# Pack attention and a channel mix on one core: a third softmax buffer, sums of weights stored in 2 KB runs, and later due times in the planner

## The chip, the cores and the metric

The kernel runs on one core of a Trainium2 chip. Its engines are TensorE (PE: matmuls, PEld: the weight loads that overlap them), VectorE (DVE), ScalarE (ACT), GpSimd (POOL) and SyncE (SP), which issues nearly all transfers. Each runs its own list of instructions in order and waits for the others by semaphores. The metric is the device time of one execution in microseconds.

## The reference

Two attentions in a row: 32 packed queries p attend to k and v, and q attends to the packed result; then a channel mix with a token shift.

```python
B, H, S, D, NP = 8, 8, 576, 64, 32;  d_model, d_ff = 512, 1024
def sm_attn(qq, kk, vv):
    s = scale * qq @ kk.transpose(0, 1, 3, 2)
    a = np.exp(s - s.max(-1, keepdims=True))
    return (a / (a.sum(-1, keepdims=True) + 1e-09)) @ vv
p_packed = sm_attn(p, k, v)
x = sm_attn(q, p_packed, p_packed)        # then (B, S, 512)
xk = mu_k * x + (1 - mu_k) * x_prev       # x_prev: x one token earlier
xr = mu_r * x + (1 - mu_r) * x_prev
v = np.maximum(xk @ w_k, 0) ** 2 @ w_v
out = v / (1 + np.exp(-(xr @ w_r)))
```

All is float32. The large products split each operand into a high and a low part and do three matmuls for one.

## The kernel before

**Stages.** Attention goes by the 8 batches of 576 rows, the channel mix by 9 blocks of 512 rows. Blocks 0 to 4 run one by one: 16 groups of gates (tiles `pr`, lines 1157 to 1159), 32 of keys (`ph`, 1090 to 1092), 32 of values (`pvo`, 1186 to 1188), where a group is three matmuls of 512 columns. Blocks 5 and 6, then 7 and 8 run as pairs (lines 1474 and 1628 to 1630): 32 groups of turned gates, then seven products instead of eight for keys and for values, 56 groups each. Those need sums of weights (`sw`), which are made on VectorE (line 1307) and ScalarE (1323) during blocks 1 to 4, stored to memory from `tmp` tiles (`sum<-sw`) and read back in the pairs into a ring of four cells: two in old k and q tiles (`ring`), two in columns of `wv_h` and `wv_l`.

**One batch of attention on PE.** Five kinds of short bursts go between groups: first scores (723, of `kT`), the product with v (745, into `pv`), the transposition of `pm` (775), second scores (879, of `qT`), and twice the last product (926, with `a`), whose result ScalarE copies into `xt` (949). Between the first scores and the product with v lies the first softmax: its exponentials are turned on VectorE into an `e` tile (`blocks`), stored (`away`) and read back (`aT`). Between second scores and last product lies the second softmax, in two halves, each in an `e` tile: turn (895), maximum (901), subtraction (903), exponential (905), sum (908), division (910 to 914), turn into `a` (918). k and q are loaded in pieces into `raw` tiles and turned on VectorE (455).

**What sets the order.** `Flow` is a planner that runs when the program is built. Each piece of work is a generator that asks for tiles (`take`, `give`), events, and time on an engine (`vec`, `act`, `pe`, `load`). Flow keeps a clock for each engine and emits next what could start earliest by its own costs, and among equals the lowest rank. The emitted order is fixed; on the chip an engine waits at an instruction until its inputs are there. The table `RANK_...` sets ranks, `BUFS` the number of tiles. `LANDS` (2.0) is the time that the planner adds to a transfer, `flow.t` the time at which a piece is ready by its clocks. A `tmp` tile (four) holds either a square on its way (`r`, 1102), a mixed `x` (1050), or a sum until its store has landed.

Of the kernel before, what the change touches and what calls it, by code (L numbers as in the profile page):

```python
# [182 lines left out]
def attn_pack_channel_mix(ctx: ExitStack, tc: tile.TileContext, q, k, v, p, mu_k, mu_r, w_k, w_v, w_r, out):  # L183
# [53 lines left out]
    def pe(us, after=None):  # L237
        return "tensor", us, after, None

    def load(dst, src, issue, us, queue="queue"):  # L240
        yield queue, issue, None, None
        dict(queue=nc.sync, scalar=nc.scalar, gpsimd=nc.gpsimd)[queue].dma_start(dst, src)  # L242
        begin = max(flow.free.get("dma", 0.0), flow.t + 0.46)
        flow.free["dma"] = begin + us
        flow.free[queue] = max(flow.free[queue], begin - 2.0)
        flow.now.t = begin + us + LANDS

    LANDS = 2.0
    T6 = S // 6
    HALVES = slice(0, 64), slice(64, P)  # L250

    def reached():
# [10 lines left out]
    ps = ctx.enter_context(tc.tile_pool(name="ps", bufs=1, space=bass.MemoryType.PSUM))  # L263
    pairs = ctx.enter_context(ExitStack())
    pp = pairs.enter_context(tc.tile_pool(name="pp", bufs=1, space=bass.MemoryType.PSUM))
    BUFS = dict(raw=3, kq=4, vt=2, pt=1, a0=1, a1=1, aT=1, pm=2, e=2, a2=1, xt=6, tmp=4, xk=NC, sq=NF, sig=4,
                pa=2, both=1, m=4, n=4, staged=4, ex=3, pair=0, ring=0, store=2, ahead=0)
    for tag, n in BUFS.items():
        flow.pool(tag, n)
    flow.slots["m"].pop()  # L270
# [3 lines left out]

    PAIRS = NB - 4, NB - 2
    MORE = {("sig", 4 + j): f"raw{j}" for j in range(3)}
    MORE.update({("sig", 7): "a20"})
    RANK_B, RANK_TURN, RANK_BACK, RANK_OUT, RANK_AHEAD, RANK_L = 4.805, 10.211, 4.545, 0.48, 25.869, 31.395
    RANK_SUMS, CHAIN, KEPT = dict(k=29.865, v=12.442), {NB - 4: 45, NB - 2: 37.468}, {NB - 4: 23.054, NB - 2: 6.114}

    def banks(slot):
        return pp.tile([P, 2, 512], F32, name="pa", tag=f"pa{slot}")
# [5 lines left out]
            const.tile([P, 1 if "m" == tag[0] or "n" == tag[0] else 2], F32, name=f"{tag}{j}", tag=f"{tag}{j}")  # L288
    for tag, n, size in (
        ("xk", NC, 2 * TB), ("sq", NF, 2 * TB), ("tmp", 4, WP), ("sig", 4, DM), ("kq", 4, S),   # L290
        ("raw", 3, S), ("a2", 1, S), ("ex", 3, TB), ("e", 2, S), ("aT", 1, 5 * P), ("vt", 2, NPR * 5 * D),
    ):
        for j in range(n):
            sb.tile([P, size], F32, name=tag, tag=f"{tag}{j}")
# [88 lines left out]
    def first_loads():  # L383
        flow.spawn(first_packed(), 5)
        for h in range(2):
            for j in (2 * h, 2 * h + 1):
                flow.spawn(first_pair(k, "kT", j, "xk"), FIRST_K[h])
                flow.spawn(first_pair(q, "qT", j, "xk" if j == NPR - 1 else "raw"), FIRST_Q[h])
            flow.spawn(values_of(0, h), FIRST_V[h])

    def loads(b):
        flow.spawn(packed(b), lrank(b) - 0.03)
        for src, tag in ((k, "kT"), (v, "vt"), (q, "qT")):
            if tag == "vt":
                for h in range(2):
                    flow.spawn(values_of(b, h), lrank(b) - 0.01)
                continue
            flow.now.rank = lrank(b) - (0.02 if tag == "kT" else 0.0)
            for pr in range(NPR):

                space = "raw"
                slot = yield from flow.take(space)
                if b < EARLY:

                    raw = tile_([P, 6, 2 * D], F32, space, slot, "raw")
                    for hh in range(2):
                        yield from load(
                            raw[:T6, :, hh * D:(hh + 1) * D], src[b, 2 * pr + hh].rearrange("(c p) d -> p c d", p=T6),
                            0.51, 0.6,
                        )  # L410
                        back_to_issue()
                    flow.spawn(transposed_on_pe(tag, b, pr, space, slot, raw), rank(b), flow.free["dma"] + LANDS)
                    continue

                raw = tile_([P, NTB, 32], F32, "raw", slot)
                for o in range(0, P, 32):
                    hh, dh = divmod(o // 32, 2)
                    yield from load(
                        raw[o:o + 32],
                        src[b, 2 * pr + hh, :, 32 * dh:32 * dh + 32].rearrange("(t tb) d -> t tb d", tb=NTB),  # L420
                        0.63, 0.41,
                    )
                    back_to_issue()
                flow.spawn(transposed(tag, b, pr, slot, raw), rank(b) if b < 3 else RANK_TURN, flow.free["dma"] + LANDS)

    def back_to_issue(queue="queue"):
        flow.now.t = flow.free[queue]
# [286 lines left out]
    def front(b):  # L714

        yield from flow.wait(("pt", b), *(("kT", b, pr) for pr in range(NPR)))
        slots = yield from two_slots()
        yield pe(1.2)
        s1 = [banks(slot) for slot in slots]
        for hf in range(2):  # L720
            for pr in range(NPR):
# [14 lines left out]
        slot = yield from flow.take("pa")  # L736
        pv = banks(slot)
        yield from flow.wait(*((tag, b, h) for tag in ("aT", "vt") for h in range(2)))
        yield pe(1.4)
        both = [(*vts.pop((b, h)), *aTs.pop((b, h))) for h in range(2)]  # L740

        def summed_up(h, c, pr, rows):
# [27 lines left out]
        flow.give("pa", slot)  # L770

        slot = yield from flow.take("pa")
        yield pe(0.21)
        pT = banks(slot).rearrange("p a b -> p (a b)")
        nc.tensor.transpose(pT[:, :P], pm.rearrange("p a b -> p (a b)"), ident)
        ppT = sb.tile([P, P], F32, name="ppT", tag="ppT")
# [93 lines left out]
    def scores(b, sp, pm, ppT, left):  # L870

        yield from flow.wait(*(("qT", b, pr) for pr in range(NPR)))
        slots = yield from two_slots()
        yield pe(1.2)
        s2 = [banks(slot) for slot in slots]
        for hf in range(2):
            for pr in range(NPR):
                for h, own in enumerate(HALVES):
                    nc.tensor.matmul(
                        s2[hf][32 * pr:32 * pr + 32, h, :HS], ppT[own, 32 * pr:32 * pr + 32],  # L880
                        ts["qT", b, pr][1][own, hf * HS:(hf + 1) * HS],
                        start=True, stop=True,
                    )
            flow.set(("s2", b, hf))
        for pr in range(NPR):
            flow.give("kq", ts.pop(("qT", b, pr))[0])
        for hf in range(2):
            flow.spawn(back(b, hf, sp, pm, slots[hf], s2[hf], left), rank(b, hf) + (RANK_BACK if b > 2 else -1))

    def back(b, hf, sp, pm, slot, s2, left):  # L890
# [27 lines left out]
        nc.vector.transpose(a2.rearrange("p (a b) -> p a b", b=32), e)  # L918
        flow.give("e", se)
        slots = yield from two_slots()  # L920
        yield pe(0.7)
        px = [banks(slot) for slot in slots]
        for pr in range(NPR):
            own = slice(32 * pr, 32 * pr + 32)
# [314 lines left out]
    def spaces():  # L1239

        flow.spawn(spaces_of_weights(), flow.now.rank)
        yield from flow.wait(("s2", B - 1, 1))
        for _ in range(2):
            slot = yield from flow.take("vt")
            feed("vt", slot)
        for _ in range(2):
            one = yield from flow.take("kq")
            two = yield from flow.take("kq")
            feed_ring("two", ("kq", one), ("kq", two))
        for _ in range(3):  # L1250
            yield from flow.take("raw")
        for j in range(3):
            flow.give("sig", 4 + j)
        yield from flow.wait(*(("room", B - 1, g) for g in range(NG)))
        flow.spawn(spaces_of_sequences(), flow.now.rank)
        yield from flow.wait(*(("xt", B - 1, c, hf) for c in range(NC) for hf in range(2)))
        yield from flow.take("a2")
        flow.give("sig", 7)
        rooms = []
        for tag, n in (("e", 2), ("aT", 1), ("a0", 1), ("a1", 1)):  # L1260
            for _ in range(n):
                slot = yield from flow.take(tag)
                rooms.append(("a", int(tag[1])) if tag in ("a0", "a1") else (tag, slot))
        yield from flow.wait("sums")
        rooms += [("ex", j) for j in range(3)]
        for j in range(0, 8, 2):
            ahead.append(("two", *rooms[j:j + 2]))
            flow.give("ahead", j // 2)

# [32 lines left out]
    def chain_of_sums(at, temps, left):  # L1302
# [5 lines left out]

        def stored(kind, dst, slot, both):
            yield from reached()  # L1310
            yield from load(dst, both, 0.5, 0.45)
            flow.give("tmp", slot)
            flow.give("store", 0)
            left[kind] -= 1
            if not left[kind]:
                flow.set("sums of keys" if kind == "k" else "sums")

        def kept(n, v):
            yield from flow.take("store")
            slot = yield from flow.take("tmp")  # L1320
            both = tile_([P, 2, HD], F32R, "tmp", slot, "sw")
            yield act(HD)
            nc.scalar.copy(both[:, 0], v)
            yield vec(HD)
            nc.vector.tensor_tensor(both[:, 1], v, both[:, 0].bitcast(F32), op=ALU.subtract)
            flow.spawn(stored(kind, sums[kind, n, k][:, :, at, :], slot, both.bitcast(F32)), flow.now.rank)

        for kind, wh, wl in (("k", wk_h, wk_l), ("v", wv_h, wv_l)):
            flow.now.rank = RANK_SUMS[kind]
# [36 lines left out]
    def arriving(i, kind, n, k, j):  # L1366
        both = ring_of(j)
        yield from reached()
        for h, half in enumerate(both):
            yield from load(half.bitcast(F32), sums[kind, SUM_OF[n], k][:, h], 0.5, 0.9)  # L1370
            if not h:
                back_to_issue()
        streamed[i, kind, n, k] = j, *both
# [466 lines left out]
```

## Time and profile before

| | us |
|---|---|
| median of 3 runs | 578.67 |
| lowest, highest | 578.11, 579.21 |
| the profiled execution | 577.32 |
| its span, first to last instruction | 575.1 |
| PE, DVE, ACT busy in the span | 558.4, 452.1, 370.5 |

The views used are the page (busy times, the costliest groups of instructions, transfers), what each engine waited for, busy time and granted clock in stretches, the chain that ended last, and the instructions in order of time. A busy PE is not PE at its peak; the granted clock of 1.00 is 2.4 GHz and 0.50 is 1.2 GHz.

### The profile page before, as it was taken

How to read it: one execution, taken by the hardware profiler on the slowest of the kernel's cores; microseconds unless marked ns; L12 is line 12 of the kernel's file. 1: busy time of each engine (PE TensorE's matmuls, PEld its weight loads, DVE VectorE, ACT ScalarE, POOL GpSimd, SP SyncE). 2: the span in 40 equal slices, each digit the busy share in tenths (PEclk: the TensorE clock that was granted, in tenths of full speed). 3: DMA queues.
4: the chain of work that ended last, by engine and by line, in shares of the span. 5: the costliest groups of instructions: out<-in, count | busy, mean ns of one | idle time of the engine just before them, and what ended most of it. 6: DMA issues, size and time to landing. Idle time of an engine off the chain costs nothing.

```text
span 575.1 us, 10286 instructions
## 1 busy us (share of the span) xinstructions
PE 558.4 (97%) x3654; PEld 433.8 (75%) x3654; DVE 452.1 (79%) x884; ACT 370.5 (64%) x673; POOL 7.2 (1%) x36
## 2 busy tenths in 40 slices
PE   8999999999999999998999999999999999999995
PEld 7867777777677776676686777778888888888884
DVE  3797799829799889947897979957389999119974
ACT  3689979435567675535754677498678737656720
POOL 4000000000000000000000000000000000000000
PEclk9999999999999999998999999999999999999998
DMA  9998856656655863876866863220352572044255
GB/s 214 279 268 248 192 122 129 175 106 135 117 157 135 175 165 89 213 198 133 181 121 197 199 168 111 79 71 0 112 181 75 148 172 46 1 146 147 74 128 92
DMA packets 225763, 81.96 MB, mean 143 GB/s; under 512 B 183592, under 2 KB 214832, under 8 KB 225712
## 3 DMA queue, kind: packets, MB, share of 16 engines
q1 hardware_dynamic: 221296, 80.38, 56.7%
q10 hardware_dynamic: 4160, 0.66, 0.6%
q8 instruction: 29, 0.48, 0.3%
q0 software_dynamic: 256, 0.26, 0.2%
q14 instruction: 22, 0.18, 0.1%
HBM read 59.90 MB, written 21.36 MB: 141 GB/s over the span
## 4 chain that ended last, share of the span: by engine, by line
PE 55%; DVE 21%; ACT 7%; DMA 7%; SPq 5%; issue 4%; DVEq 0%; ACTq 0%
PE ph L1474 27%; SPq L242 5%; DMA raw<-in_q 3%; DVE x L1054 3%; PE ph L1090 3%; PE pr L1628 3%; PE pr L1629 3%; PE pr L1630 3%; PE ph L1091 2%; PE ph L1092 2%; DMA raw<-in_k 2%; PE pvo L1186 2%; PE pvo L1187 1%; PE pvo L1188 1%; PE pr L1157 1%
## 5 line engine op out<-in xcount | busy, mean ns | idle before, releaser
L1186 PE MATMUL pvo<-wv_h,sq 128*128 128x512 f32 x160 | 64.2, 401 | 1.3 <-ACT r L1102 1.3
L1090 PE MATMUL ph<-xk,wk_h 128*128 128x512 f32 x160 | 64.5, 403 | 0.0
L1091 PE MATMUL ph<-xk,wk_h 128*128 128x512 f32 x160 | 62.6, 392 | 0.0
L1092 PE MATMUL ph<-xk,wk_l 128*128 128x512 f32 x160 | 62.6, 391 | 0.0
L1187 PE MATMUL pvo<-wv_l,sq 128*128 128x512 f32 x160 | 62.4, 390 | 0.0
L1188 PE MATMUL pvo<-wv_h,sq 128*128 128x512 f32 x160 | 62.4, 390 | 0.0
L1050 ACT ACTIVATE x<-xt,mus 128x64 f32<-128x64 f32 (+7 forms) x92 | 42.4, 512 | 12.2 <-DMA out<-x 5.6
L1102 ACT ACTIVATE r<-ph 128x512 f32<-128x512 f32 x40 | 23.8, 595 | 37.1 <-PE ph L1092 25.4
L1054 DVE SCALAR_TENSOR_TENSOR x<-xt,mus,x 128x64 f32<-128x64 f32 (+7 forms) x92 | 41.5, 493 | 6.9 <-ACT x L1050 6.9
L1186 PEld LDWEIGHTS pvo<-wv_h,sq 128*128 128x128 f32 x160 | 30.1, 188 | 12.9 <-issue 4.5
L949 ACT COPY xt<-pa 128x576 f32<-128x576 f32 x28 | 32.9, 1262 | 9.9 <-PE pa L926 9.7
L1090 PEld LDWEIGHTS ph<-xk,wk_h 128*128 128x128 f32 x160 | 30.2, 189 | 11.6 <-issue 4.1
L1474 PE MATMUL ph<-vB,wv_h 128*128 128x512 f32 x116 | 36.2, 393 | 0.0
L1092 PEld LDWEIGHTS ph<-xk,wk_l 128*128 128x128 f32 x160 | 30.2, 188 | 6.4
L1188 PEld LDWEIGHTS pvo<-wv_h,sq 128*128 128x128 f32 x160 | 30.0, 188 | 6.5
L1474 PE MATMUL ph<-vT,ring 128*128 128x512 f32 x138 | 34.5, 392 | 0.0
L1091 PEld LDWEIGHTS ph<-xk,wk_h 128*128 128x128 f32 x160 | 30.2, 189 | 5.6
L1187 PEld LDWEIGHTS pvo<-wv_l,sq 128*128 128x128 f32 x160 | 30.1, 188 | 5.7
L1168 ACT ACTIVATE sig<-pr 128x512 f32<-128x512 f32 x36 | 20.8, 601 | 15.1 <-PE pr L1159 7.9
L1474 PEld LDWEIGHTS ph<-vT,ring 128*128 128x128 f32 x138 | 25.9, 188 | 5.8
L455 DVE STREAM_TRANSPOSE qT<-raw 128x576 f32<-128x576 f32 x28 | 21.5, 772 | 10.3 <-DMA raw<-in_q 10.2
L1071 ACT CAST xr<-x 128x512 fp32r<-128x512 f32 x32 | 19.8, 619 | 14.3 <-DVE x L1054 13.9
(211 smaller groups left out, 1351.8 us busy)
## 6 DMA issues: line engine op xcount, KB each, us to landing
sum<-sw SPq DMA_DIRECT2D x32, 256.0 KB, 2.7
ring<-sum SPq DMA_DIRECT2D x32, 256.0 KB, 3.0
raw<-in_k SPq DMA_DIRECT2D x112, 72.0 KB, 2.8
raw<-in_q SPq DMA_DIRECT2D x112, 72.0 KB, 2.8
out<-sig SPq DMA_DIRECT2D x20, 256.0 KB, 3.0
st<-in_moe_w_k SPq DMA_DIRECT2D x8, 512.0 KB, 5.5
st<-in_moe_w_v SPq DMA_DIRECT2D x8, 512.0 KB, 5.4
wv_h<-sum SPq DMA_DIRECT2D x16, 256.0 KB, 3.9
```

The source lines that it names most:

```text
L242: dict(queue=nc.sync, scalar=nc.scalar, gpsimd=nc.gpsimd)[queue].dma_start(dst, src)
L949: nc.scalar.copy(*in_order(b, xt[:, :, 1 + hf * HS:1 + (hf + 1) * HS], xt[:, :, 1:].rearrange("p c (t a b) -> p c a b t", a=2, t=32)[:, :, ...
L1050: nc.scalar.mul(x32[:, o:o + n], xts[b, c][:, 1 + s:1 + s + n], mus[:, j, c:c + 1])
L1054: nc.vector.scalar_tensor_tensor(x32[:, o:o + n], xts[b, c][:, s:s + n], mus[:, j + 1, c:c + 1], x32[:, o:o + n], op0=ALU.mult, op1=ALU.add,)
L1090: nc.tensor.matmul(ph, wk_h[:, c, fs], xh, start=(c == 0), stop=False)
L1091: nc.tensor.matmul(ph, wk_h[:, c, fs], xl, start=False, stop=False)
L1092: nc.tensor.matmul(ph, wk_l[:, c, fs], xh, start=False, stop=(c == NC - 1))
L1102: nc.scalar.activation(r, ph, AF.Relu)
L1186: nc.tensor.matmul(pv[t], sh, wv_h[:, f, :], start=(n == 0), stop=False)
L1187: nc.tensor.matmul(pv[t], sh, wv_l[:, f, :], start=False, stop=False)
L1188: nc.tensor.matmul(pv[t], sl, wv_h[:, f, :], start=False, stop=(n == NF - 1))
L1474: nc.tensor.matmul(bank[2], w, x, start=(not more and step == k == 0), stop=(step == 2 and k == count - 1), skip_group_check=True,)
```

## The change

It adds and removes no arithmetic. An `e` tile is added (`e=3`). The store of a sum writes 2 KB in one run (`sums[kind, n, k][:, at]`) where it wrote two runs of 1 KB, and the read back takes two runs of 1 KB where it took one of 2 KB. Up to three stores are out at once (`store=3`), each booked 0.9 us in the planner instead of 0.45. Transposes of k and q of batches from 3 on are ready 1.2 us later in the planner (`LATER`), and the bursts of these batches 0.8 us later than their inputs (`MARGIN`). The first batch's q goes into `sq` tiles instead of `raw`. In the pairs a fifth `tmp` tile is an old `ex` tile. Eight ranks change.

```diff
+    def burst(us, b):
+        return "tensor", us, flow.t + (MARGIN if b > 2 else 0.0), None
     LANDS = 2.0
+    LATER, MARGIN = 1.2, 0.8
-    BUFS = dict(..., e=2, ..., store=2, ahead=0)
+    BUFS = dict(..., e=3, ..., store=3, ahead=0)
-    MORE.update({("sig", 7): "a20"})
-    RANK_B, RANK_TURN, RANK_BACK, RANK_OUT, RANK_AHEAD, RANK_L = 4.805, 10.211, 4.545, 0.48, 25.869, 31.395
-    RANK_SUMS, CHAIN, KEPT = dict(k=29.865, v=12.442), {NB - 4: 45, NB - 2: 37.468}, {NB - 4: 23.054, NB - 2: 6.114}
+    MORE.update({("sig", 7): "a20", ("tmp", 4): "ex2"})
+    RANK_B, RANK_TURN, RANK_BACK, RANK_OUT, RANK_AHEAD, RANK_L = 4.805, 7.611, 3.04, 0.581, 27.568, 39.997
+    RANK_SUMS, CHAIN, KEPT = dict(k=37.759, v=10.564), {NB - 4: 45, NB - 2: 37.468}, {NB - 4: 23.054, NB - 2: 5.269}
-                flow.spawn(first_pair(q, "qT", j, "xk" if j == NPR - 1 else "raw"), FIRST_Q[h])
+                flow.spawn(first_pair(q, "qT", j, "xk" if j == NPR - 1 else "sq"), FIRST_Q[h])
-                flow.spawn(transposed(...), rank(b) if b < 3 else RANK_TURN, flow.free["dma"] + LANDS)
+                flow.spawn(transposed(...), rank(b) if b < 3 else RANK_TURN, flow.free["dma"] + LANDS + (LATER if b > 2 else 0.0))
         # first scores, product with v, transposition of pm, second scores, last product
-        yield pe(1.2)
+        yield burst(1.2, b)
...
-        for tag, n in (("e", 2), ("aT", 1), ("a0", 1), ("a1", 1)):
+        for tag, n in (("e", 3), ("aT", 1), ("a0", 1), ("a1", 1)):
...
-        yield from flow.wait("sums")
-        rooms += [("ex", j) for j in range(3)]
         for j in range(0, 8, 2):
+            if j == len(rooms):
+                yield from flow.wait("sums")
+                rooms += [("ex", j) for j in range(2)]
+                flow.give("tmp", 4)
...
-            yield from load(dst, both, 0.5, 0.45)
+            yield from load(dst, both, 0.5, 0.9)
-            flow.spawn(stored(kind, sums[kind, n, k][:, :, at, :], slot, both.bitcast(F32)), flow.now.rank)
+            flow.spawn(stored(kind, sums[kind, n, k][:, at], slot, both.bitcast(F32)), flow.now.rank)
-            yield from load(half.bitcast(F32), sums[kind, SUM_OF[n], k][:, h], 0.5, 0.9)
+            yield from load(half.bitcast(F32), sums[kind, SUM_OF[n], k][:, :, h], 0.5, 0.9)
```

The lists of instructions are the same up to batch 2's last products, and PE's is the same again from the pairs' turned gates on, apart from which tiles hold what. In between, three places. On PE at batch 5, in block 3's keys, from the product with v to the second scores, before:

```order
L745 MATMUL pa<-vt,aT 32x64 x40
L1090 MATMUL ph<-xk,wk_h 128x512
L1091 MATMUL ph<-xk,wk_h 128x512
L1092 MATMUL ph<-xk,wk_l 128x512
L775 MATMUL pa<-ident,pm 128x128
L1090 MATMUL ph<-xk,wk_h 128x512
L1091 MATMUL ph<-xk,wk_h 128x512
L1092 MATMUL ph<-xk,wk_l 128x512
L879 MATMUL pa<-qT,ppT 32x288 x16
```

and on PE at the same place after the change, from the product with v on:

```order
L749 MATMUL pa<-vt,aT 32x64 x40
L1094 MATMUL ph<-xk,wk_h 128x512
L1095 MATMUL ph<-xk,wk_h 128x512
L1096 MATMUL ph<-xk,wk_l 128x512
L1094 MATMUL ph<-xk,wk_h 128x512
L1095 MATMUL ph<-xk,wk_h 128x512
L1096 MATMUL ph<-xk,wk_l 128x512
L779 MATMUL pa<-ident,pm 128x128
```

The transposition of pm has two groups ahead of it instead of one; the second scores follow after three more groups instead of one.

SP at batch 5, around the stores of the turned exponentials (`away`) and of sums, before:

```order
L242 DMA sum<-sw 256x1x256 x2
L242 DMA away<-blocks 128x576 x2
L242 DMA raw<-in_q 32x18x32 x7
L242 DMA aT<-away 32x4x160 x2
L242 DMA aT<-away 32x4x128 x4
L242 DMA aT<-away 32x4x160 x2
L242 DMA sum<-sw 256x1x256 x2
```

and SP at the same place after the change:

```order
L245 DMA away<-blocks 128x576 x2
L245 DMA raw<-in_q 32x18x32
L245 DMA sum<-sw 128x512 x2
L245 DMA raw<-in_q 32x18x32 x3
L245 DMA pin<-in_p 32x4x32
L245 DMA aT<-away 32x4x160 x2
L245 DMA aT<-away 32x4x128 x4
L245 DMA aT<-away 32x4x160 x2
L245 DMA sum<-sw 128x512 x2
```

Two stores of sums stand behind one load of q after `away` instead of seven, and two still stand behind the eight reads of `aT`.

VectorE at batch 5, the last rows ahead of pm (`sq` are squares, `rs` the divisor of the first softmax), before:

```order
L455 STREAM_TRANSPOSE qT<-raw 128x576
L1109 CAST sq<-r 128x512
L1111 TENSOR_TENSOR sq<-r,sq 128x512
L1325 TENSOR_TENSOR sw<-sw 128x256
L763 TENSOR_SCALAR rs<-sm 128x2
L1307 TENSOR_TENSOR sw<-sw 128x256
L765 RECIPROCAL rs<-rs 128x2
L1109 CAST sq<-r 128x512
L769 TENSOR_TENSOR pm<-pa,rs 128x128
```

and VectorE at the same place after the change:

```order
L459 STREAM_TRANSPOSE qT<-raw 128x576
L1113 CAST sq<-r 128x512
L1331 TENSOR_TENSOR sw<-sw 128x256
L1115 TENSOR_TENSOR sq<-r,sq 128x512
L1313 TENSOR_TENSOR sw<-wv_h,wv_l 128x256 x2
L1313 TENSOR_TENSOR sw<-sw 128x256
L1331 TENSOR_TENSOR sw<-sw 128x256
L767 TENSOR_SCALAR rs<-sm 128x2
L1313 TENSOR_TENSOR sw<-wv_h,wv_l 128x256
L769 RECIPROCAL rs<-rs 128x2
L532 STREAM_TRANSPOSE pt<-pin 128x128
L1313 TENSOR_TENSOR sw<-sw 128x256
```

This fence ends two rows short: a cast of a square and pm follow. Five more rows of other work stand between the last transpose of q and pm; in both lists the row just ahead of pm is a cast of a square.

## Rows read from the trace of the kernel before

**Rows 1.** The page: busy us (share of span) xinstructions; one costly group (busy, mean ns).

```profile
PE 558.4 (97%) x3654; PEld 433.8 (75%) x3654; DVE 452.1 (79%) x884; ACT 370.5 (64%) x673; POOL 7.2 (1%) x36
...
L949 ACT COPY xt<-pa 128x576 f32<-128x576 f32 x28 | 32.9, 1262 | 9.9 <-PE pa L926 9.7
```

**Rows 2.** What PE waited for, 128 to 376 us: us in total, times, longest.

```profile
PE pa L775 <- DVE pm L769: 2.8, 2, 1.7
PE pvo L1186 <- ACT r L1102: 1.1, 1, 1.1
PE pa L926 <- DVE a L918: 0.8, 1, 0.8
PE pa L926 <- DVE m L912: 0.7, 1, 0.7
PE pr L1157 <- DVE sig L1197: 0.7, 1, 0.7
PE pa L745 <- DMA aT<-away: 0.6, 1, 0.6
PE pa L926 <- ACT a L803: 0.4, 1, 0.4
```

**Rows 3.** Stretches: us, busy PE, PEld, DVE, ACT, POOL (x), PEclk, DMA share, GB/s.

```profile
425.00:450.00 25.00, 25.00 (x111) 20.57 (x110) 25.00 (x44) 19.75 (x37) 0.00 (x0) 1.00 0.33 96
...
260.00:262.00 2.00, 1.50 (x12) 0.82 (x20) 2.00 (x7) 0.34 (x2) 0.00 (x0) 0.73 0.80 188
262.00:264.00 2.00, 2.00 (x33) 0.56 (x29) 1.45 (x3) 0.91 (x2) 0.00 (x0) 0.50 0.70 120
264.00:266.00 2.00, 2.00 (x12) 1.69 (x9) 0.68 (x1) 0.61 (x2) 0.00 (x0) 0.92 0.80 194
```

**Rows 4.** In order of time around PE's longest stop: start, us, instruction, idle before.

```profile
259.81 0.43 DVE L1109 CAST sq<-r 128x512 fp32r<-128x512 f32 x1 [3.95 <-ACT r L1105]
260.16 0.28 DVE L769 TENSOR_TENSOR pm<-pa,rs 128x128 f32<-128x128 f32 x1
...
260.50 0.33 PE L775 MATMUL pa<-ident,pm 128*128 128x128 f32 x1 [1.66 <-DVE pm L769]
```

**Rows 5.** Who waited for transfers, 128 to 376 us: us, times, longest.

```profile
DVE qT L455 <- DMA raw<-in_q: 10.2, 12, 1.9
ACT r L1102 <- DMA sum<-sw: 9.8, 4, 5.8
```

**Rows 6.** SP's queue in order of time ahead of that stop.

```profile
245.88 5.31 SPq L242 DMA_DIRECT2D raw<-in_q  x7
251.24 3.94 SPq L242 DMA_DIRECT2D aT<-away  x8
255.28 1.23 SPq L242 DMA_DIRECT2D sum<-sw  x2
```

**Rows 7.** The page's transfers: issues, KB each, median us from issue to landing.

```profile
sum<-sw SPq DMA_DIRECT2D x32, 256.0 KB, 2.7
ring<-sum SPq DMA_DIRECT2D x32, 256.0 KB, 3.0
...
wv_l<-sum SPq DMA_DIRECT2D x16, 256.0 KB, 4.1
...
away<-blocks SPq DMA_DIRECT2D x12, 288.0 KB, 2.5
```

**Rows 8.** SP's queue in the first pair's keys, in order of time.

```profile
408.27 1.76 SPq L242 DMA_DIRECT2D ring<-sum  x4
413.72 0.37 SPq L242 DMA_DIRECT2D wv_h<-sum  x1
```

**Rows 9.** VectorE in order of time, the first half of batch 7's second softmax.

```profile
352.23 1.45 DVE L895 STREAM_TRANSPOSE e<-pa 128x576 f32<-128x576 f32 x2
...
365.43 0.79 DVE L918 STREAM_TRANSPOSE a<-e 128x576 f32<-128x576 f32 x1
```

**Rows 10.** The chain that ended last, one piece: a table load on ScalarE.

```profile
241.69 1.28 ACT L1168
```

More of the change, by code (lines that the diff above doesn't have):

```diff
@@ L265, in attn_pack_channel_mix @@
     pp = pairs.enter_context(tc.tile_pool(name="pp", bufs=1, space=bass.MemoryType.PSUM))
-    BUFS = dict(raw=3, kq=4, vt=2, pt=1, a0=1, a1=1, aT=1, pm=2, e=2, a2=1, xt=6, tmp=4, xk=NC, sq=NF, sig=4,
-                pa=2, both=1, m=4, n=4, staged=4, ex=3, pair=0, ring=0, store=2, ahead=0)
+    BUFS = dict(raw=3, kq=4, vt=2, pt=1, a0=1, a1=1, aT=1, pm=2, e=3, a2=1, xt=6, tmp=4, xk=NC, sq=NF, sig=4,
+                pa=2, both=1, m=4, n=4, staged=4, ex=3, pair=0, ring=0, store=3, ahead=0)
     for tag, n in BUFS.items():
@@ L290, in attn_pack_channel_mix @@
         ("xk", NC, 2 * TB), ("sq", NF, 2 * TB), ("tmp", 4, WP), ("sig", 4, DM), ("kq", 4, S),
-        ("raw", 3, S), ("a2", 1, S), ("ex", 3, TB), ("e", 2, S), ("aT", 1, 5 * P), ("vt", 2, NPR * 5 * D),
+        ("raw", 3, S), ("a2", 1, S), ("ex", 3, TB), ("e", 3, S), ("aT", 1, 5 * P), ("vt", 2, NPR * 5 * D),
     ):
@@ L423, in loads @@
                     back_to_issue()
-                flow.spawn(transposed(tag, b, pr, slot, raw), rank(b) if b < 3 else RANK_TURN, flow.free["dma"] + LANDS)
+                flow.spawn(transposed(tag, b, pr, slot, raw), rank(b) if b < 3 else RANK_TURN, flow.free["dma"] + LANDS + (LATER if b > 2 else 0.0))
     def back_to_issue(queue="queue"):
@@ L738, in front @@
         yield from flow.wait(*((tag, b, h) for tag in ("aT", "vt") for h in range(2)))
-        yield pe(1.4)
+        yield burst(1.4, b)
         both = [(*vts.pop((b, h)), *aTs.pop((b, h))) for h in range(2)]
@@ L772, in front @@
         slot = yield from flow.take("pa")
-        yield pe(0.21)
+        yield burst(0.21, b)
         pT = banks(slot).rearrange("p a b -> p (a b)")
@@ L873, in scores @@
         slots = yield from two_slots()
-        yield pe(1.2)
+        yield burst(1.2, b)
         s2 = [banks(slot) for slot in slots]
@@ L920, in back @@
         slots = yield from two_slots()
-        yield pe(0.7)
+        yield burst(0.7, b)
         px = [banks(slot) for slot in slots]
```

## The prediction

> **What bounds the kernel now.** I read the busy times first. TensorE (PE) is busy for 558.4 of the 575.1 us of the span, VectorE (DVE) for 452.1 and ScalarE (ACT) for 370.5 [rows 1], so only what stops PE, or slows its clock, can be won. The second view is what PE itself waited for, from 128 us (where the two orders first part) to 376 us (from where PE no longer idles until the tail). Its seven rows sum to 2.8 + 1.1 + 0.8 + 0.7 + 0.7 + 0.6 + 0.4 = 7.1 us in eight waits [rows 2]. The third view is the granted clock: it reads 0.73, 0.50 and 0.92 in three stretches of 2 us from 260 us on, that is the lower level, 1.2 GHz instead of 2.4, for about 3.4 us; lost are 2 x (0.27 + 0.50 + 0.08) = 1.7 us [rows 3]. PE had idled 0.6 and 1.7 us shortly before [rows 2]. So the change can give at most 7.1 + 1.7 = 8.8 us, unless it also shortens the parts whose order it leaves alone (the first 128 us, and PE's order from the pairs' gates to the end).
>
> Both versions issue 2907 matmuls, and the same number of every kind of VectorE row. PE's price for what lies between bursts: 111 matmuls in 25.00 us, or three (one group, a plain step of the channel mix) in 0.68 us [rows 3].
>
> **Where the largest stall comes from.** Before the longest stop (1.66 us at 260.50), PE waits for VectorE's pm (260.16); that stands in VectorE's queue behind the cast of a square (259.81), which waited 3.95 us for ScalarE's r [rows 4]. ScalarE waited up to 5.8 us, 9.8 us in four waits, for stores of sums to land, since r needs one of four tmp tiles and the stores hold them [rows 5]. The stores themselves were late on SP's queue: seven loads of q (5.31 us) and eight of aT (3.94 us) were issued before two stores went out at 255.28 [rows 6]. The stops for r (1.1) and for pm (2.8 in two) are one chain.
>
> **The change, part by part.**
>
> *Stores of sums, A.* What hangs on them: 1.1 + 2.8 + 1.7 of clock = 5.6 us [rows 2, 3]. The planner now books 0.9 us for a store instead of 0.45, allows three stores at once, and SP's order at batch 5 has one load of q instead of seven between away and the next two stores: six issues at 5.31 / 7 = 0.76 us, so 4.5 us earlier [rows 6]. Two further stores still stand behind aT's eight loads. PE's transposition of pm comes two groups after the pv burst instead of one there, two to seven elsewhere where it was one to three; each group more covers 0.68 us of lateness. pm still stands behind one cast of a square. I take 4.5 of the 5.6: one wait of the smaller size (1.1) stays.
>
> The 2 KB runs: 32 stores of 1 KB runs land in a median of 2.7 us; the nearest store with long runs, away (288 KB, 2304 bytes in a run), in 2.5, while reads in 2 KB runs (ring) take 3.0 [rows 7]. So a store gains between nothing and 0.2 us, four waits at most 0.8 together; I take 0, since the order decides. The Trainium skill ("DMA: Bandwidth & Descriptors", "Why small descriptors are slow (HBM only)") speaks against this edit: it gives a packet about three cycles of fixed cost, 8 data cycles per 256 bytes, so 1 KB to 2 KB would save some 4% of the transfer, an estimate from that page. By it the sum is the one I use; by away's row it would be up to 0.8 us better.
>
> *Reads of sums.* Their runs fall from 2 KB to 1 KB. The nearest row is the reads into wv's columns, already 1 KB runs on chip: 4.1 us instead of 3.0 [rows 7]. A ring cell is refilled while one product of 8 groups (8 x 0.68 = 5.4 us) runs: four loads issued from 408.27 to 410.03, the next product at 413.72 [rows 8]. The first cell's last load then lands near 409.15 + 4.1 = 413.3, the second's at 414.1, wanted at 413.72 and 414.40. It fits by 0.3 us; wv's cells run like that today without a wait. I take 0. If they land 0.5 us later still, 0.2 to 0.4 us is lost at each of six tight refills (three a pair), up to 2.4 us.
>
> *Bursts and transposes later, and the third e buffer, B.* The other burst waits are 0.8 + 0.7 + 0.6 + 0.4 = 2.5 us [rows 2]. VectorE waited 10.2 us in twelve waits (longest 1.9) for q's loads [rows 5]; the transposes, booked 1.2 us later, now stand behind rows that have their data, and bursts of batches from 3 on are booked 0.8 us later. These are planner's times: nothing on the chip waits for them, they only move rows, at no cost while other groups fill PE. With three e buffers both halves of a second softmax go through VectorE side by side. Of 2.5 I take 1.8 and leave 0.7, at the seam of batch 7: there the trace has 28 rows from e (352.23) to the end of a (366.22), 14.0 us or 0.50 each, and PE waited 0.7 [rows 9, 2]. After, 24 rows (12.0 us) meet 20 groups (13.6 us) plus the scores' burst, but behind four products with sig.
>
> *Later batches.* Scores of batches 5, 6 and 7 move from groups 269, 328, 375 to 278, 347, 400, and the last burst from 417 to 425; the pairs' products, which need its banks, open at group 432. Seven groups, 4.8 us, must hold two copies of 1.26 us each [rows 1]. Cover is left: 2.3 us; with the old 15 groups it was 7.7. I take 0, and 0.8 us for a new wait of the common size somewhere among the crowded rows.
>
> *The rest.* Two more table loads on ScalarE, 1.28 us each [rows 10], hidden by its 64% share [rows 1]; at worst 2.6 us. The first q in sq tiles moves waits from loads of k to loads of weights on SP: 0. The fifth tmp tile and the other ranks in the pairs: 0, as PE does not wait there now. The wait for sig (0.7 in rows 2) is untouched.
>
> **Sum.** 4.5 + 1.8 - 0.8 = 5.5 us. Against its own execution 577.32 - 5.5 = 571.8; the three runs have their median at 578.67, 1.35 above the profiled one, so 573.2 us.
>
> **Rivals.**
>
> *The chain comes back (slower).* With three stores allowed, three of four tmp tiles can be held, and each r behind them stops ScalarE, then the cast, then pm. One recurrence of the great stop costs 1.7 + 1.7 of clock = 3.4 us [rows 2, 3]. The trace holds one such stop. If it comes at each of batches 4, 5 and 6, 10.2 us stand where 3.4 did, with the two 1.1 waits kept: 6.8 lost, 2.5 of B won, 578.67 + 4.3 = 583.0 us. It decides from two recurrences on (3.4 - 2.5 = +0.9, 579.6). For it: aT's loads still precede two stores. Against: pm has more cover everywhere, and the stores start sooner.
>
> *It comes back once.* A then gives 2.2; 2.2 + 1.8 - 0.8 = 3.2, so 575.5 us.
>
> *The gain is given back in the pairs (same).* Six refills late (2.4) and the table loads exposed (2.6): 5.5 - 5.0 = 0.5, so 578.2 us. For it: 0.3 us of slack. Against: wv's cells.
>
> *It does not do what it says.* The due times do not bind the chip: if q's loads land as late against the new order, A and B shrink by half, 573.2 + 3.1 = 576.3 us.
>
> **How the numbers follow.** Forecast 0.55, once back 0.15, not as said 0.06, same 0.11, slower 0.13. A measurement of this kernel tells 0.2%, 1.2 us, from no change. Faster 0.55 + 0.15 + 0.06 = 0.76; same 0.11; slower 0.13. Low end: all 8.8 us and the runs' half width of 0.55, 578.67 - 9.3 = 569.4. High end: through the case of no gain, 579.2, which leaves out the slower case and little else.
>
> **What would show it.** Right: PE's waits from 128 us to the seam sum to 2 to 4 us, the granted clock stays at 1.00 between start and tail, ScalarE's waits for stores of sums fall well under 9.8 us and VectorE's for q under 5. Wrong in A: a stop of over 1 us before the transposition of pm, with a cast behind r ahead of it, and a stretch at 1.2 GHz. Wrong on the reads: PE waits of ring tiles after 390 us. Wrong on the seam: a wait at the first product of the pairs, or bursts waiting for a. The whole forecast fails if new waits between 128 and 376 us sum to more than 8.8 us, or PE's order in the pairs hides less than it does now.

## The result, and the profile after the change

| | before | after |
|---|---|---|
| median, us | 578.39 (4 runs) | 570.77 (4 runs) |
| lowest, highest | 576.95, 579.21 | 569.78, 574.29 |
| the profiled execution | 577.32 | 569.78 |
| its span | 575.1 | 567.6 |
| PE waits, 128 to 376 us | 7.1 | 2.1 |

The ratio is 0.9882, 95% interval 0.9835 to 0.9929: 7.6 us faster, where 5.5 were forecast. The page of the changed kernel, with the lines that answer to [rows 1]:

```profile
span 567.6 us, 10280 instructions
PE 556.7 (98%) x3654; PEld 434.5 (77%) x3654; DVE 452.0 (80%) x884; ACT 371.4 (65%) x675; POOL 7.2 (1%) x36
```

The engines do the same work, but for two more table loads on ScalarE; the span is 7.5 us shorter. What PE waited for between 128 and 376 us (us in total, times, longest), to be read against [rows 2]:

```profile
PE pa L727 <- DVE kT L459: 0.7, 1, 0.7
PE pa L930 <- DVE a L922: 0.6, 2, 0.3
PE pr L1161 <- DVE sig L1201: 0.5, 1, 0.5
PE pa L779 <- DVE pm L773: 0.3, 1, 0.3
```

Nothing is left of the wait at r, of the one for `aT`, or of the seam; pm fell from 2.8 to 0.3, and one wait is new: 0.7 us for a turned k at the scores of batch 7. The clock (columns as in [rows 3]) now holds through the stretch that had the dip, and through the whole middle:

```profile
256.00:266.00 10.00, 10.00 (x146) 7.29 (x145) 6.57 (x20) 4.74 (x11) 0.00 (x0) 1.00 0.66 151
...
128.00:376.00 248.00, 245.91 (x1866) 186.20 (x1865) 221.43 (x474) 160.80 (x293) 0.82 (x8) 1.00 0.64 154
376.00:558.00 182.00, 182.00 (x808) 148.59 (x809) 132.17 (x218) 119.25 (x211) 0.00 (x0) 1.00 0.38 100
```

The accounts of the two profiled executions: 7.1 - 2.1 = 5.0 us of waits; 1.7 us of clock; and of PE's waits ahead of 128 us, 3.6 before and 2.9 after, 0.7. That is 7.4 of the 7.5 us. It is an account of one execution of each kernel, and of the changed one's fastest. The dip in particular is not typical of the kernel before: this execution has a mean granted clock of 0.994, the traces of this case without a dip ahead of the tail have 0.996 to 0.999, and of the 48 runs of the kernel before that were timed beside the experiments 38 have 0.996 or more. Of what the 7.6 us between the medians consist is not shown run by run.

One view does not fit the forecast. ScalarE's waits for stores of sums, which were 9.8 us at r [rows 5] and 3.0 at x, are still there:

```profile
ACT sw L1329 <- DMA sum<-sw: 7.5, 4, 3.2
ACT r L1106 <- DMA sum<-sw: 4.0, 4, 2.2
ACT x L1054 <- DMA sum<-sw: 1.8, 1, 1.8
```

They sum to 13.3 us against 12.8. PE's waits went away although ScalarE's did not. The place of the old 1.66 us stop, batch 5, tells how (start, us, instruction, idle before and what ended it; SP, ScalarE, VectorE, PE in turn):

```profile
250.04 4.32 SPq L245 DMA_DIRECT2D aT<-away  x8
254.46 0.85 SPq L245 DMA_DIRECT2D sum<-sw  x2
...
256.69 0.41 ACT L1329 CAST sw<-sw 128x256 fp32r<-128x256 f32 x1 [2.54 <-DMA sum<-sw]
257.00 1.08 ACT L1106 ACTIVATE r<-ph 128x512 f32<-128x512 f32 x2
...
258.85 0.42 DVE L1113 CAST sq<-r 128x512 fp32r<-128x512 f32 x1
259.18 0.28 DVE L773 TENSOR_TENSOR pm<-pa,rs 128x128 f32<-128x128 f32 x1
...
257.32 1.37 PE L749 MATMUL pa<-vt,aT 128*32 128x64 f32 x80
258.62 0.50 PE L1094 MATMUL ph<-xk,wk_h 128*128 128x512 f32 x1
...
260.12 0.27 PE L779 MATMUL pa<-ident,pm 128*128 128x128 f32 x1
```

Two stores still stand behind the eight reads of `aT`, as in [rows 6], and ScalarE still stops for them. But counted from the first group behind the pv burst (258.62 here), which stood in the kernel before at

```profile
257.88 0.50 PE L1090 MATMUL ph<-xk,wk_h 128*128 128x512 f32 x1
```

the stores go out 1.6 us sooner (4.2 us ahead of it instead of 2.6), pm is finished 1.7 us sooner (0.8 us after it instead of 2.6), and PE has two groups to do in that time instead of one (0.68 us more). The stop of 1.66 is less than 1.7 + 0.7, so it is gone, though by little: pm ended at 259.46, PE wanted it at 260.12.

### The profile page after: what moved, and what is told of

It reads as the page before. It is cut to its first block, busy times and chain, and to the rows that moved or that the text cites. A ratio compares the mean times of both kernels' runs of the same rounds, so it can differ in the third digit from the quotient of the medians.

```text
span 567.6 us, 10280 instructions
## 1 busy us (share of the span) xinstructions
PE 556.7 (98%) x3654; PEld 434.5 (77%) x3654; DVE 452.0 (80%) x884; ACT 371.4 (65%) x675; POOL 7.2 (1%) x36
## 4 chain that ended last, share of the span: by engine, by line
PE 68%; DVE 17%; ACT 8%; DMA 3%; issue 2%; SPq 0%; DVEq 0%; POOL 0%; ACTq 0%; POOLq 0%
PE ph L1480 27%; PE ph L1094 4%; PE pvo L1190 4%; PE ph L1095 4%; PE ph L1096 4%; PE pvo L1191 3%; PE pvo L1192 3%; DVE x L1058 3%; PE pr L1634 3%; PE pr L1635 3%; PE pr L1636 3%; PE spare L1817 2%; PE pr L1161 1%; DMA st<-in_moe_w_k 1%; PE pr L1162 1%
## 5 line engine op out<-in xcount | busy, mean ns | idle before, releaser
L1190 PEld LDWEIGHTS pvo<-wv_h,sq 128*128 128x128 f32 x160 | 30.0, 188 | 12.2 <-issue 4.0
L1480 PE MATMUL ph<-vT,wv_h 128*128 128x512 f32 x116 | 36.1, 392 | 0.0
L1113 DVE CAST sq<-r 128x512 fp32r<-128x512 f32 x40 | 16.4, 411 | 14.2 <-ACT r L1109 14.0
L1115 DVE TENSOR_TENSOR sq<-r,sq 128x512 fp32r<-128x512 f32 x40 | 26.9, 676 | 0.2
L1161 PE MATMUL pr<-wr_h,xr 128*128 128x512 f32 x64 | 25.8, 403 | 0.5 <-DVE sig L1201 0.5
```

The source lines that it names most:

```text
L1115: nc.vector.tensor_tensor(hl[:, 1, :], r, hl[:, 0, :].bitcast(F32), op=ALU.subtract)
L1161: nc.tensor.matmul(pr, xh[:, ts_], wr_h[:, c, :], start=(c == 0), stop=False)
L1190: nc.tensor.matmul(pv[t], sh, wv_h[:, f, :], start=(n == 0), stop=False)
L1480: nc.tensor.matmul(bank[2], w, x, start=(not more and step == k == 0), stop=(step == 2 and k == count - 1), skip_group_check=True,)
```

## Experiments

Every group of runs was timed beside runs of the kernel before; their medians were 579.40, 579.25 and 579.20 us in the three groups.

| kernel | order of the instructions | median, us | ratio to before, interval |
|---|---|---|---|
| before, fifth tmp tile | as before | 578.14 | 0.9977 (0.9965 to 0.9990) |
| before, stores on GpSimd's queue | as before | 572.98 | 0.9889 (0.9871 to 0.9907) |
| before, 2 KB runs | as before | 577.37 | 0.9962 (0.9946 to 0.9978) |
| before, due times later | its own | 580.37 | 1.0016 (1.0001 to 1.0031) |
| after, again | as after | 571.80 | 0.9883 (0.9852 to 0.9915) |
| after, 1 KB runs | as after | 573.83 | 0.9907 (0.9887 to 0.9928) |
| after, stores on GpSimd's queue | as after | 566.56 | 0.9777 (0.9757 to 0.9797) |
| after, no later due times | its own | 573.21 | 0.9892 (0.9872 to 0.9913) |
| after, two e tiles | its own | 589.48 | 1.0177 (1.0153 to 1.0201) |
| after, stores booked as before | its own | 575.74 | 0.9939 (0.9918 to 0.9961) |
| after, ranks of before | its own | 573.74 | 0.9911 (0.9892 to 0.9929) |
| after, GpSimd's queue, no later due times | as the one without due times | 571.34 | 0.9862 (0.9844 to 0.9881) |

"As before" means that PE, VectorE and ScalarE have the same list word for word, so that only the chip's side changes. An edit of the planner's numbers, by contrast, makes a new order everywhere behind it.

**What holds ScalarE: too few tiles?** A fifth `tmp` tile exists that the planner does not know of:

```diff
         slot = yield "slot", tag
+        if tag == "tmp":
+            free = min(self.room)        # of five, the one given back first
+            self.room.remove(free)
+            self.at[slot] = free[1]
         return slot
...
-                flow.spawn(first_pair(q, "qT", j, "xk" if j == NPR - 1 else "raw"), FIRST_Q[h])
+                flow.spawn(first_pair(q, "qT", j, "xk" if j == NPR - 1 else "sq"), FIRST_Q[h])
```

(The second edit is the change's own. A first q takes 768 columns of a raw tile, raw's other uses 576; without it three raw tiles give back 576 columns, the size of one e tile and more than one tmp tile. What the prediction filed under "the rest" makes the room.)

> The kernel before, its order unchanged on every engine: the planner still counts four tmp tiles, but five exist and are used in turn (the first batch's q goes into sq tiles, which makes the room). So an r or an x finds a tile while stores of sums are on their way. Theory (the chain of held tmp tiles is what stops PE): ScalarE's wait of r for stores of sums falls from 9.8 us to under 3, the two stops ahead of the transposition of pm (1.1 and 1.7 us) and the one at r (1.1) go, the clock stays at 1.00 from 128 us to the tail, and 0.6 us of the start's waits for raw go: 4 to 6 us faster than the kernel before, 572.5 to 574.5. Rival (PE waits because pm stands late in VectorE's own order, whoever holds tiles): the waits at pm stay over 2 us in sum, at most 1.5 us faster, 577 or more.

1.3 us faster by the medians; the rival's bound was 1.5. What ScalarE waited for, then PE:

```profile
ACT r L1111 <- DMA sum<-sw: 5.4, 1, 5.4
...
PE pr L1166 <- DVE sig L1206: 1.7, 1, 1.7
PE pvo L1195 <- ACT r L1111: 1.5, 1, 1.5
PE pa L784 <- DVE pm L778: 1.4, 2, 0.9
PE pa L732 <- DVE kT L464: 1.2, 1, 1.2
```

pm's wait is halved (2.8 to 1.4), but sig and kT wait in its stead, and one r still stands 5.4 us. One more tile lets ScalarE run on to the next wait for the same late stores. The number of tiles is worth 1.3 us here, not the 4 to 6 of the theory.

**Or the stores' place on SP's queue?** The same order again, but GpSimd issues the 32 stores, which does next to nothing else there:

```diff
-            yield from load(dst, both, 0.5, 0.45)
+            yield from load(dst, both, 0.5, 0.45, real=nc.gpsimd)
```

> The kernel before, its order unchanged, but the 32 stores of sums are issued by GpSimd's queue instead of SP's, so none stands behind loads of q or reads of aT. Theory (step A as predicted: stores are late on SP's queue, that is where the stall comes from): ScalarE's waits for stores of sums fall from 9.8 + 3.0 us to under 6, PE's stops at r and pm lose 2 to 5.6 us, 573 to 576.5. Rival (the landing of a store, not its place in the queue, holds the tile): waits of r within 20% of before, within 1 us of the kernel before. Third: GpSimd's issue takes longer and stores land over 1 us later than the 2.7 us of before: slower, 579 to 583.

6.4 us faster, at the upper edge of step A's theory. ScalarE:

```profile
ACT r L1102 <- DMA sum<-sw: 3.3, 1, 3.3
```

PE, in the same execution:

```profile
PE pa L745 <- DMA aT<-away: 2.8, 2, 1.5
PE pa L926 <- DVE m L912: 0.7, 1, 0.7
PE pvo L1186 <- ACT r L1102: 0.6, 1, 0.6
PE pa L775 <- DVE pm L769: 0.5, 1, 0.5
```

r and pm, 3.9 us together in [rows 2], are down to 1.1. (This execution took 574.55 us, 1.6 more than the median of its kernel. The dip of the clock behind its waits for `aT`, below, is not typical: its mean granted clock is 0.994, that of the other four 0.997 to 0.999.) The third theory is out: the stores land in a median of 3.2 us instead of 2.7, which is less than they gain in front of the queue. From the end of the sum's second half on VectorE to its store's issue, added over all 32, the trace of before has 62.2 us, this one 15.6. The Trainium skill ("Trainium Kernel Development and Optimization", "Key Constraints") says that issuing transfers from several engines "only saves the sequencer's issue time". The trace agrees in so far as a store no longer stands behind the issue of loads. A second thing goes with it: no load stands behind a store whose sum is not ready. SP's queue had stood idle in front of a store for 11.8 us in four places before (and for 17.8 in seven in the first trace of the changed kernel), by the gaps between its issues; here no store is on it. How the 6.4 us divide between the two was not tried.

**The 2 KB runs alone.**

```diff
-... sums[kind, n, k][:, :, at, :], slot, both.bitcast(F32)) ...
+... sums[kind, n, k][:, at], slot, both.bitcast(F32)) ...
-... load(half.bitcast(F32), sums[kind, SUM_OF[n], k][:, h], 0.5, 0.9)
+... load(half.bitcast(F32), sums[kind, SUM_OF[n], k][:, :, h], 0.5, 0.9)
```

> The kernel before with nothing but the layout of the sums in memory changed: stores write runs of 2 KB instead of 1 KB, reads into the ring take runs of 1 KB instead of 2 KB. Order unchanged on every engine. Prediction: no difference, 578.4 within 0.6 us; a store lands up to 0.2 us sooner (2.5 to 2.7 us), a read in 3.0 to 4.1 us. Rival 1: the runs help the stores, ScalarE's waits for them (9.8 us) fall by 0.8 us or more, 577.6. Rival 2: the reads are late in the pairs, PE waits for ring tiles up to 2.4 us, 579 to 581.

2.0 us faster by the medians, 1.3 to 3.1 by the interval, where I had taken 0 and at most 0.8. The landing is not shorter: a median of 2.9 us, against 2.7 [rows 7]. What is shorter is SP's time for the issue (ns, min/median/max). Of the kernel before:

```profile
L242 SPq DMA_DIRECT2D sum<-sw x32: 513/567/1943, 172.7 to 353.0; - x32
L242 SPq DMA_DIRECT2D ring<-sum x4: 344/382/382, 351.2 to 352.6; - x4
```

and with 2 KB runs:

```profile
L242 SPq DMA_DIRECT2D sum<-sw x32: 319/377/1704, 174.0 to 355.3; - x32
L242 SPq DMA_DIRECT2D ring<-sum x4: 561/562/582, 352.6 to 354.6; - x4
```

An issue with half the runs takes 0.19 us less, one with twice as many 0.18 us more. The stores are issued while SP is crowded; the reads while it is idle, and PE has no wait for a ring tile in any of these traces. That the gain comes from the shorter issue is argued, not shown: the profiled execution took 578.83 us, 1.5 more than the median of its kernel, and PE waits 7.9 us in it between 128 and 376 us where it waited 7.1 before.

**The due times alone.** The kernel before with `LATER` and `MARGIN`, all else as before:

> The kernel before with nothing but the due times: transposes 1.2 us and bursts 0.8 us later in the planner for batches from 3 on (e=2, stores and ranks as before). Theory (the three parts need each other): the burst waits of 128 to 376 us fall from 7.1 us to under 3.5, the clock stays up, but the last batch moves from group 417 to 432, where the pairs' products begin and no group covers it: a wait of 2 to 5 us at that seam, so 575 to 580. Rival (the due times are the whole gain): 570.5 to 572. Second rival (a planner's due time does nothing on the chip): 578 within 1 us.

Slower by 1 us. The burst waits are nearly gone (1.1 us before 376 us), and the seam takes it all back. PE behind 376 us:

```profile
PE pa L930 <- DVE a L922: 4.0, 1, 4.0
PE ph L1478 <- ACT xt L953: 1.9, 1, 1.9
PE pa L930 <- ACT xt L953: 1.4, 1, 1.4
```

Batch 7's last bursts both stand at group 432, where no group covers them, and the granted clock is 0.50 for some 10 us from 387 us on. The wait at the seam, 7.3 us, is over the 2 to 5 that I had put down.

**The changed kernel again**, to see which of its waits are its own:

> The changed kernel again, unchanged, as the measure for the others of this group: 570.8 within 0.8 us, 1.2 to 1.5% under the kernel before. If its waits of 2.1 us between 128 and 376 us belong to the order, the same four places wait again (scores of batch 7, sig, pm of batch 5, products with a); if they are chance, others do.

571.8 (570.5 to 575.78). The four places are the same (kT waits 0.6 us and sig 0.5, much as in the first execution), the other two with other sizes:

```profile
PE pa L930 <- DVE a L922: 1.0, 1, 1.0
PE pa L779 <- DVE pm L773: 0.8, 1, 0.8
```

(This pm is batch 6's, not batch 5's as expected; of the two waits for `a` in the first execution the one at 203 us is missing.) They belong to the order; how long each lasts does not. In this execution the 32 stores wait 61.5 us for their issue, in the first one 50.0: the change does not bring them forward reliably.

**The changed kernel with 1 KB runs.** The diff above, undone.

> The changed kernel with the old layout of the sums (stores in runs of 1 KB, reads of 2 KB), its order unchanged on every engine. By the prediction: within 0.6 us of the changed kernel, 570.2 to 571.4, since the order does the work. Rival, after the kernel before gained 2.0 us by this layout alone: the long runs are a part of the gain of their own, and this is 1.5 to 2.5 us slower than the changed kernel, 572.3 to 573.3, with ScalarE's waits for stores (13.3 us) up by 1 us or more.

2.0 us by the medians, which the rival had; the intervals of the two ratios overlap, so by the times alone it is not certain. The waits say the same: ScalarE's for stores are 17.5 us, where the two traces with 2 KB runs have 13.3 and 16.3, the 32 stores wait 69.5 us for their issue instead of 50.0 and 61.5, and PE waits 4.9 us instead of 2.1 and 2.9. PE's largest:

```profile
PE pa L779 <- DVE pm L773: 1.6, 2, 0.9
PE pa L930 <- DVE a L922: 1.5, 1, 1.5
```

**The changed kernel, stores on GpSimd's queue.** `real=nc.gpsimd`, as above.

> The changed kernel with the 32 stores of sums issued by GpSimd's queue, order unchanged. Theory (the change lets PE go on while ScalarE still waits 13.3 us for stores, so the place of the stores no longer matters to PE): at most 1.5 us better, 569.3 to 570.8, though ScalarE's waits for stores fall under 8 us. Rival 1 (SP's queue is still what ends the remaining waits): all 2.1 us go, 568.5 or less. Rival 2 (SP, free of the stores, brings k and q earlier and the reads of aT collide with the stores, as the 2.8 us of waits for aT in the kernel before with GpSimd's queue): 572 to 574.

Rival 1, and more: 566.56 us, 5.2 under the changed kernel, 2.2% under the kernel before, and the fastest of all; its four runs lie between 566.32 and 566.78, where the ten of the changed kernel lie between 569.78 and 575.78. PE has not one wait from 84 us to the tail; its busy time between 128 and 376 us is the whole stretch:

```profile
128.00:376.00 248.00, 248.00 (x1880) 188.90 (x1879) 222.79 (x477) 164.03 (x297) 18.68 (x42) 1.00 0.64 154
```

ScalarE waits for a store once, 1.9 us. My theory, that the stores' place no longer mattered to PE, falls: the waits left were still theirs. The gain is even larger than those waits. Of the 3.9 us between the spans of the changed kernel's second trace (568.8) and this one (564.9), 2.7 are idle time of PE and 1.2 busy time; the latter stays open.

**Without later due times.** `LATER, MARGIN = 0.0, 0.0` in the changed kernel:

> The changed kernel with LATER and MARGIN at zero: transposes and bursts are due as soon as the planner has their inputs (batch 5's second scores move from group 278 to 270, batch 6's from 347 to 329). Theory (step B: late due times keep rows that lack data off VectorE and PE): VectorE waits for q's loads 4 us or more again (0 in the changed kernel, 10.2 before), PE's burst waits rise by 2 to 4 us, 573 to 575. Rival (due times are not needed once the stores are booked at their true cost and a third e exists): within 1 us of the changed kernel, 570 to 571.8.

573.21: 1.4 us slower by the medians, the theory's lower edge, and the intervals overlap. VectorE does wait for q again, 5.7 us in five waits; PE's waits are 3.4 us in seven places, the largest:

```profile
PE pa L727 <- DVE kT L459: 1.5, 1, 1.5
PE pa L930 <- DVE pm L773: 0.7, 1, 0.7
```

The same with the stores on GpSimd's queue:

> The changed kernel with stores of sums on GpSimd's queue and, of that version, LATER and MARGIN at zero (the order of the kernel without due times). Theory (due times keep rows that wait for q off VectorE, whoever issues the stores, as q's own loads take most of SP's time): 1 to 2 us slower than the 566.6 us with due times, 567.6 to 568.6, VectorE waiting 3 us or more for q. Rival (due times only cover what the stores' issue took from q's loads): 566.6 within 0.5 us.

571.34, 4.8 us slower than with due times (the intervals of the two ratios do not overlap): more than the theory's 1 to 2, and against the rival. VectorE waits 4.0 us for q. So the due times are not a cover for the stores; they are worth more once the stores are out of the way. The span of this execution is 4.6 us longer (569.5 against 564.9). PE idles for 3.0 of them (7.3 against 4.3 us). Of the other 1.6, some 1.2 lie inside two bursts of the last product, which count as busy: from their starts at 297.38 and 370.93 to the next group they take 1.23 and 1.53 us, where the fourteen bursts with due times take 0.67, but for one of 0.78.

**Two e tiles.** The changed kernel with `e=2` (and four tmp in the pairs):

> The changed kernel with two e tiles instead of three (and, with them, no fifth tmp tile in the pairs); due times, stores and ranks as changed, so the planner makes another order: batch 7's last bursts both stand at group 432, where the pairs begin. Theory (the third e is what pays for late due times): burst waits before 376 us stay under 3 us, but at the seam PE waits as it did with late due times alone (4.0 + 1.4 + 1.9 us), 577 to 580. Rival (the third e is of no use, VectorE sets the pace of a second softmax): 571 to 572.5.

Much slower, 589.48 us. The stretch at the seam, PE in order of time:

```profile
385.82 1.20 PE L883 MATMUL pa<-qT,ppT 64*32 64x288 f32 x32
395.92 1.27 PE L930 MATMUL pa<-a,pm 32*64 32x288 f32 x16 [8.91 <-DVE a L922]
398.56 2.32 PE L930 MATMUL pa<-a,pm 32*64 32x288 f32 x16 [1.37 <-ACT xt L953]
402.80 0.79 PE L1478 MATMUL ph<-wk_h 128*128 128x512 f32 x1 [1.92 <-ACT xt L953]
```

12.2 us of waits, and a granted clock of 0.50 for some 17 us from 391 us on; the middle adds 3.1 us of waits at r and a dip of 3.4 us behind them. The mechanism was right, the size too small (7.3 us of seam expected, and no price for the clock): batch 7's second scores now stand at group 432 too, so its whole second softmax lies bare. Late due times need the third e, and the third e takes its room from the first q's move.

**Booking and ranks.** The changed kernel with `store=2` and 0.45 in the planner:

> The changed kernel with stores booked as before in the planner (two at once, 0.45 us each), the new layout kept. The order changes: batch 7's last bursts move from groups 420 and 425 to 428 and 432. Theory (booking is a part of the chain's cure): ScalarE's waits for stores and PE's waits at r or pm grow, and the seam waits 1 to 3 us: 573 to 576. Rival (the booking does nothing on the chip): 570.5 to 572.

575.74, in the theory's range, but only half by its way. The seam waits 2.4 us (the last burst is at group 432), with a dip of 3.4 us behind it. But ScalarE's waits for stores did not grow (11.4 us against 13.3 and 16.3), the stores wait 49.6 us for their issue, no more than in the changed kernel, and PE waits 0.7 us at pm and not at r; its other waits in the middle are 1.5 for sig and 1.6 for ppT. The booking sets the order, not how soon the stores go out. And with the eight old ranks:

> The changed kernel with the ranks of before. Bursts stand within six groups of the changed kernel's from batch 5 on. Theory (the ranks only reshuffle what the other parts make possible): within 1 us of the changed kernel, 570.5 to 572.5. Rival (the ranks carry the cure, as one stop at pm after a held r costs 1 to 3 us): 573 to 576, with a stop of over 1 us ahead of a transposition of pm.

573.74: the rival's time, though the interval overlaps the changed kernel's, and without the stop that the rival named. Ahead of a transposition of pm PE waits 0.3 us; its waits are 4.0 us before 376 us and 1.0 behind it, none over 1.1, and ScalarE's r is again held longest:

```profile
ACT r L1106 <- DMA sum<-sw: 11.1, 4, 5.0
```

Taken away one at a time, the third e, the booking, the ranks, the 2 KB runs and the due times cost 17.7, 3.9, 1.9, 2.0 and 1.4 us, 26.9 in all, where all of them together gain 7.6. They are not terms of a sum: each removal but that of the runs makes another order, and that order's weak place sets the price.

## Why the prediction was right, point by point

**The bound.** PE's waits and the clock were all that could be won: 7.1 + 1.7 = 8.8 us. Won, in the two profiled executions, were 5.0 + 1.7 there, and 0.7 ahead of 128 us, which I had left out. Whether that last is chance is open: with the first q in `sq` tiles, PE idled between 2 and 20 us for 0.3 to 2.4 us (under 1.3 in nine of ten traces), and without that edit for 1.1 to 2.0 in four. (The traces record 3654 matmuls in either kernel, not 2907; that the number is the same is what the argument needs.)

**A, the chain through r and pm.** Forecast 4.5 of 5.6; measured 5.3 (no wait at r, 0.3 at pm, no dip). The size came out, in part by luck: 1.7 us of it are the dip, which about a fifth of the executions of the kernel before have. Of the reasons, two held: pm's cover on PE, and that the stops start at the stores on SP's queue, which the run with GpSimd's queue on the order of before shows (6.4 us). A third held at one place alone: "six issues at 5.31 / 7 = 0.76 us, so 4.5 us earlier". At batch 5 the two stores behind the reads of `aT` had waited 7.8 and 8.2 us for their issue; after the change those behind the reads wait 4.9 and 4.2, those behind the one load of q 2.0 and 2.4, and ScalarE's longest stop there fell from 5.8 to 2.5 us. But over all 32 stores the delay was 62.2 before and 50.0 and 61.5 after, and the sign "ScalarE's waits for stores of sums fall well under 9.8 us" did not come: 13.3 us stand, mostly at the copy of the next sum (`sw`) instead of r. I counted the loads that were moved away in front of one pair of stores, and not those that stand in front of the others. Nor are the stops "one chain": they lie at 209.83 (r), 218.89 and 260.50 us (pm), and ahead of the second ScalarE had waited for a store with an x, 0.8 us at 217.14, not with an r.

**The 2 KB runs.** The mis-sized term: 0 taken, up to 0.8 allowed, about 2 measured on either order (certain on the order of before, likely on the other). I priced the landing, by the nearest rows, and the landing did not shorten; nor does the 4% show that the prediction estimates from the Trainium skill ("DMA: Bandwidth & Descriptors", "Why small descriptors are slow (HBM only)"). The cost that did fall is SP's time for an issue, which the same trace would have given: a median of 567 ns for a store with two runs to a partition, 382 for a read with one. That the 2 us come from there is the likely reading, not a shown one.

**Reads of sums.** 0 taken, 0 measured: no PE wait stands behind them. They land in 3.9 us instead of 3.0, close to the 4.1 that I took from wv's rows, but not for the reason I gave. With 1 KB runs on the order of before the same reads land in 3.1 us, and with 2 KB runs on the changed order in 3.9: it goes with the order, not with the runs.

**B and the new wait.** Burst waits other than A's and sig fell from 2.5 to 0.6 us, 1.9 against 1.8 forecast, and one new wait of 0.75 against 0.8. VectorE waits for q no more (10.2 us before, none after). The seam holds: the first product of the pairs does not wait. That it holds by the third e was not in the prediction, which gave e a line; the run with two e puts 17.7 us on it, and the run with due times alone 7.3 us of seam.

**Rivals.** The chain did not come back at several batches, though ScalarE is stopped as long as before: at batch 5, what stands behind a held tile had its result ready early enough. The runs of the changed kernel at 574 to 576 us may be executions where one stop does come back with a dip of the clock; the one at 574.29 has a mean granted clock of 0.991 instead of 0.997, which is 3.4 of its 4.5 us. It has no trace, so that stays open.

## What to carry over

When an engine waits for a buffer, look at who holds it, and whether that store was late to land or late to be issued: here a quiet engine's queue for the 32 stores was worth 6.4 us on the old order and 5.2 on the new, and one more buffer 1.3. Price a transfer's layout on the queue that issues it too, by the rows of issues with one run and with two. And an order tuned as a whole is judged as a whole: later due times lose 1 us on the old order, without the third buffer, and with it gain 4.8 where the stores are on GpSimd's queue (1.4, within the noise, where they are not).

## What the runs showed of the hardware

The clock's dip does not follow from the length of the stops alone. Four executions have two stops within 4 us at batch 5. Before, 0.60 and 1.66 us brought the clock to 0.50 [rows 2, 3]. With 2 KB runs 1.15 and 1.56 us did not:

```profile
256.00:258.00 2.00, 1.06 (x34) 0.52 (x32) 1.15 (x5) 0.00 (x0) 0.00 (x0) 1.00 0.75 223
258.00:260.00 2.00, 1.74 (x51) 1.19 (x51) 0.00 (x0) 0.32 (x1) 0.00 (x0) 1.00 0.61 192
260.00:262.00 2.00, 0.43 (x3) 0.35 (x3) 1.03 (x3) 1.20 (x3) 0.00 (x0) 1.00 0.40 63
```

and with the stores on GpSimd's queue 1.47 and 1.28 us did:

```profile
258.00:260.00 2.00, 1.59 (x49) 1.28 (x50) 0.00 (x0) 0.00 (x0) 0.00 (x0) 0.57 0.31 49
260.00:262.00 2.00, 2.00 (x6) 1.56 (x7) 1.98 (x6) 0.28 (x2) 0.34 (x1) 0.58 0.62 96
```

So a dip seen in a single trace need not be a cost of its order: 2.7 us of stops left the clock alone once and halved it once. (In the fourth, with the fifth tmp tile, stops of 0.94 and 0.93 us left it alone too.) What decides was not tried. The second thing is the price of an issue. For the same 256 KB on SP's queue it is, on the order of before, a median of 377 and 382 ns with one run to a partition and 562 and 567 with two. On GpSimd's queue a store has the same step, 688 ns with two runs (the order of before) and 539 with one (the changed kernel):

```profile
L242 POOL DMA_DIRECT2D sum<-sw x32: 682/688/997, 173.7 to 350.3; - x32
L245 POOL DMA_DIRECT2D sum<-sw x32: 539/539/819, 175.2 to 314.0; - x32
```
